# Another order for 1634 steps: linear attention and SwiGLU on one core

## The chip, the core and the metric

The kernel runs on one core of a Trainium2 chip. Six instruction streams work beside each other: TensorE (PE, with PEld for its weight loads), VectorE (DVE), ScalarE (ACT), GpSimd (POOL) and SyncE (SP), which here issues nearly all DMAs. The metric is the device time of one execution in microseconds. Three runs of the kernel before took 539.15 to 539.32 us, with a median of 539.2.

## The reference

Two stages are computed, the second from the first's output:

```python
def _attn_ref(q, k, v, alpha):                 # q, k, v, alpha: (4, 8, 768, 48)
    state = np.zeros((B, H, D, D), dtype=np.float32)
    for t in range(S):
        state = alpha[:, :, t, :, None] * state + np.einsum('bhd,bhe->bhde', k[:, :, t], v[:, :, t])
        y[:, :, t] = np.einsum('bhd,bhde->bhe', q[:, :, t], state)
    return y

def _moe_ref(x, w_gate, w_val, w_out):         # weights are float64: 384 x 1536, 384 x 1536, 1536 x 384
    g = x @ w_gate
    silu = g * (1.0 / (1.0 + np.exp(-g)))
    return (silu * (x @ w_val) @ w_out).astype(np.float32)

def reference(...):
    attn_out = _attn_ref(q, k, v, alpha)
    x = attn_out.transpose(0, 2, 1, 3).reshape(3072, 384)
    return _moe_ref(x, moe_w_gate, moe_w_val, moe_w_out)
```

## The kernel before

**Stage one: gated linear attention.** The 3072 tokens are 16 units of 192 tokens (four to a batch), each with all 8 heads, and a unit has three chunks of 64 tokens. For a unit u the loads La, Lk, Lq bring alpha, k and q and V*u*.i the values. The first units are turned on PE (T*, out of a copy widened by p*: pa, pk, pq), later ones by VectorE (tr, tk, tq). G and f are scans along time (backward and forward, lines 471 and 480). mk multiplies k by the backward scan (line 889 or 892), q multiplies q by the forward one into the tile X (line 496), and qc copies X's odd rows. K turns k for the chunks (PE, line 521), kc copies it (ACT, lines 525 and 526). C is a chunk's running sum (PE, line 597, the tile A), and ad copies it into V for the next chunk (line 620). S are the scores (PE, line 565), ma masks them (line 606), Y gives the output (PE, lines 658 and 659). From unit 4 on one step Z does scores, carry and the output of the unit before. yh and yl split the output into a high and a low part, and xr moves both into the tile xT by DMA: ten pieces a unit (line 745). xT holds 384 tokens, that is two units.

**Stage two: the MLP.** The tokens are 8 blocks of 384, d_ff is 12 slices of 128; a step s is one block and one slice, 96 in all. g and v are the two products (PE, line 760, nine matmuls each, since each operand is a high and a low part and three of the four products are taken), sl is the silu (ACT), h the product of both (DVE), hh and hl split it (ACT; then line 781 on DVE or POOL), and o adds into three banks of output rows (PE, line 793, nine matmuls). At a block's end ot copies three tiles of rows out of PSUM (line 805) and os stores them (line 818); the very last tile is stored by ACT (oz, line 809).

**Weights and checks.** Weights arrive as 64-bit words: wl loads a group, v0 to v2 cut it to 32 bits (line 162 on ACT), a and p split it. wr loads a weight slice again (384 KB) and wc checks its range; Lc and ck do so with alpha. The verdict is a flag, and behind the main path each engine loads it (line 1131) and branches to a general path that isn't taken here.

**What sets the order.** A string ORDER holds one word a step: the engine's letter (t PE, v DVE, s ACT, g POOL, y SP), the step's name, and behind @ the numbers of the PSUM banks that it takes. A loop walks it under a manual schedule:

```python
for word in ORDER.split():
    e, name = word.split(":")
    name, *banks = name.split("@")
    todo.pop(name)(engines[e], *(BANKS[int(x)] for x in "".join(banks)))
```

So each engine's queue, the buffers that the pools hand out, and the eight semaphores on which SP's transfers report in turn all follow from the order of the words. Nothing else is scheduled: an instruction waits at the head of its queue until its inputs and buffers are there.

Of the kernel before, what the change touches and what calls it, by code (L numbers as in the profile page):

```python
# [44 lines left out]
s:first y:La0 s:pa0 y:wl0 v:w0v0 t:Ta0@53 v:w0v1 s:ea0 y:Lq0 s:pq0 t:Tq0@03 v:G0 y:La1 y:V0.2 v:w0v2 s:pa1 v:f0 y:Lk1  # L45
s:pk1 t:Ta1@41 y:Lk0 t:Tk1@75 g:pk0 v:q0 s:ea1 y:V0.1 y:La2 y:Lq1 t:Tk0@60 v:mk0 y:wl1 y:V0.0 y:V0.3 s:ek1 s:pq1
t:K0.0@6 s:pa2 v:G1 s:kc0.0 g:w0a t:K0.1@4 t:Tq1@25 t:K0.2@6 v:mk1 t:C0.0@3 y:V0.4 s:w1v0 s:kc0.1 s:ad0.0 s:cq1 v:f1
g:w0p g:qc0 t:K1.2@7 t:C0.1@1 y:V0.5 t:S0@24 v:w1v1 v:ma0.1 v:ma0.0 y:wl3 v:ma0.2 y:V1.1 s:ad0.1 s:kc0.2 g:vc0 s:w3v0
t:C0.2@0 t:K1.1@3 t:K1.0@5 g:q1 y:La3 y:wl2 y:Lq2 s:ad0.2 v:de1 s:kc1.1 s:qc1 v:w3v1 v:w2v0 t:Y0@62 v:w1v2 t:S1@40
# [1114 lines left out]
```

## Time and profile before

| | us |
|---|---|
| median of three runs | 539.2 |
| the profiled execution | 539.45 |
| its span (first to last instruction) | 537.6 |
| PE busy | 525.5 (98%) |
| DVE busy | 398.7 (74%) |
| ACT busy | 244.8 (46%) |
| POOL busy | 138.8 (26%) |

The span is what the trace shows of the profiled execution; the 1.85 us by which its time is longer lie around it. Busy times count an engine's own work; the engines run beside each other, so the sums overlap. The costliest groups on PE are the MLP's: g 166.2, v 166.5 and o 257.4 us (160.5 with hh and 96.9 with hl). In the rows further down, "idle before" is the time in which the engine stood still just ahead of an instruction, and the arrow names what ended it.

### The profile page before, as it was taken

The page shows a single profiled execution, that of the slowest core. Times are in us where ns is not written, and L with a number is a line of the kernel's source. Part 1 is how long each engine was busy: PE and PEld are TensorE (multiplying, and loading weights), DVE is VectorE, ACT ScalarE, POOL GpSimd, SP SyncE. Part 2 cuts the span into 40 slices and gives each one's busy share as a digit, 9 for nine tenths or more (in the row PEclk, how much of TensorE's full clock was granted, in tenths as well). Part 3 has the DMA queues.
Part 4 walks back from the last instruction along what each step waited for, and adds up shares of the span by engine and source line. Part 5 has one row for each costly group of instructions (what it writes and reads, how often), then busy time and mean ns, then how long its engine had stood idle before and what let it go on. Part 6 is the DMA issues. An engine that isn't in the chain of part 4 may idle for free.

```text
span 537.6 us, 13527 instructions
## 1 busy us (share of the span) xinstructions
PE 525.5 (98%) x5346; PEld 514.2 (96%) x5346; DVE 398.7 (74%) x767; ACT 244.8 (46%) x573; POOL 138.8 (26%) x140
## 2 busy tenths in 40 slices
PE   5999999999999999999999999999999999999997
PEld 4789999999999999999999999999999999999996
DVE  7999999999999988988788777879856564212223
ACT  4999744443222234333242634533345553355333
POOL 8524143465233242101412014201012120110000
PEclk9999999999999999999999999999999999999999
DMA  8899767557358475765515757356264542424101
GB/s 241 222 314 243 200 194 219 135 132 202 86 145 227 101 183 125 184 156 131 147 44 145 186 132 197 82 144 176 66 164 132 140 109 62 134 53 119 52 1 48
DMA packets 96178, 77.60 MB, mean 144 GB/s; under 512 B 33264, under 2 KB 93040, under 8 KB 96112
## 3 DMA queue, kind: packets, MB, share of 16 engines
q1 hardware_dynamic: 95968, 76.52, 54.0%
q8 instruction: 43, 0.70, 0.6%
q14 instruction: 23, 0.19, 0.1%
q10 hardware_dynamic: 144, 0.20, 0.1%
HBM read 62.52 MB, written 5.90 MB: 127 GB/s over the span
## 4 chain that ended last, share of the span: by engine, by line
PE 95%; ACT 2%; DMA 1%; issue 0%; SPq 0%; DVE 0%; ACTq 0%
PE ops L793 28%; PE v L760 28%; PE g L760 28%; PE s L565 2%; PE c L680 2%; PE pt L418 1%; PE y L658 1%; PE y L659 1%; PE c L584 1%; DMA Le<-in_q_dram 1%; PE kps L521 1%; PE y L680 1%; PE A L597 1%; ACT V L620 0%; PE xp L731 0%
## 5 line engine op out<-in xcount | busy, mean ns | idle before, releaser
L760 PE MATMUL v<-xT,w 128*128 128x384 f32 x864 | 166.5, 336 | 0.0
L760 PE MATMUL g<-xT,w 128*128 128x384 f32 x864 | 166.2, 336 | 0.0
L793 PE MATMUL ops<-w,hh 128*128 128x384 f32 x576 | 160.5, 336 | 0.0
L760 PEld LDWEIGHTS v<-xT,w 128*128 128x128 f32 x864 | 150.8, 188 | 0.7 <-issue 0.3
L760 PEld LDWEIGHTS g<-xT,w 128*128 128x128 f32 x864 | 150.8, 188 | 0.3
L781 POOL TENSOR_TENSOR hl<-h,hh 128x384 fp32r<-128x384 f32 x58 | 61.8, 1067 | 275.8 <-ACT hh L776 269.6
L772 DVE TENSOR_TENSOR h<-h,v 128x384 f32<-128x384 f32 x96 | 53.1, 553 | 98.5 <-PE v L760 82.8
L793 PEld LDWEIGHTS ops<-w,hh 128*128 128x128 f32 x576 | 105.7, 188 | 0.3
L768 ACT ACTIVATE h<-g 128x384 f32<-128x384 f32 x96 | 47.0, 489 | 128.3 <-PE g L760 102.5
L776 ACT CAST hh<-h 128x384 fp32r<-128x384 f32 x96 | 48.9, 511 | 111.9 <-DVE h L772 59.8
L793 PE MATMUL ops<-w,hl 128*128 128x384 f32 x288 | 96.9, 336 | 0.0
L540 DVE STREAM_TRANSPOSE K<-Gs 32x192 f32<-32x192 f32 (+1 forms) x192 | 67.9, 353 | 4.7 <-POOL Gs L892 1.2
L793 PEld LDWEIGHTS ops<-w,hl 128*128 128x128 f32 x288 | 54.1, 188 | 0.0
L346 POOL TENSOR_TENSOR w<-t,w 128x768 fp32r<-128x768 f32 (+1 forms) x15 | 25.4, 1699 | 37.7 <-ACT w L342 37.6
L606 DVE TENSOR_TENSOR X<-s,mask 64x384 f32<-64x384 f32 (+1 forms) x48 | 26.4, 552 | 5.2 <-PE s L565 4.5
L480 DVE TENSOR_TENSOR_SCAN AT<-AT,back 128x771 f32<-128x771 f32 x16 | 29.2, 1827 | 0.6
L471 DVE TENSOR_TENSOR_SCAN Gs<-AT,inj 128x772 f32<-128x772 f32 x16 | 28.4, 1774 | 0.2
L781 DVE TENSOR_TENSOR hl<-h,hh 128x384 fp32r<-128x384 f32 x38 | 21.6, 574 | 8.9 <-ACT hh L776 8.5
L319 ACT ACTIVATE wc<-wc,wbias 128x384 f32<-128x384 f32 x36 | 23.4, 649 | 1.2
L629 DVE TENSOR_TENSOR V<-c,V 48x96 f32<-48x96 f32 x84 | 21.3, 254 | 1.9
L496 POOL TENSOR_TENSOR X<-trq,AT 112x768 f32<-112x768 f32 x9 | 15.6, 1737 | 25.5 <-DMA xT<-X 14.8
L892 POOL TENSOR_TENSOR Gs<-trk,Gs 128x768 f32<-128x768 f32 x9 | 15.3, 1697 | 23.1 <-DVE Gs L471 11.5
(121 smaller groups left out, 525.4 us busy)
## 6 DMA issues: line engine op xcount, KB each, us to landing
xT<-X SPq DMA_DIRECT2D x84, 72.0 KB, 2.2
raw<-in_moe_w_gate_dram SPq DMA_DIRECT2D x12, 384.0 KB, 4.7
raw<-in_moe_w_val_dram SPq DMA_DIRECT2D x12, 384.0 KB, 5.9
raw<-in_moe_w_out_dram SPq DMA_DIRECT2D x12, 384.0 KB, 5.7
wc<-in_moe_w_val_dram SPq DMA_DIRECT2D x12, 384.0 KB, 3.6
wc<-in_moe_w_gate_dram SPq DMA_DIRECT2D x12, 384.0 KB, 4.1
wc<-in_moe_w_out_dram SPq DMA_DIRECT2D x12, 384.0 KB, 3.6
ac<-in_alpha_dram SPq DMA_DIRECT2D x16, 288.0 KB, 3.7
```

The source lines that it names most:

```text
L319: nc.scalar.activation(dev, dev, AF.Relu, bias=wbias, scale=-1.0, accum_out=wviol[:, 0, i : i + 1])
L346: eng.tensor_tensor(out=lo, in0=src, in1=hi.bitcast(F32), op=ALU.subtract)
L471: nc.vector.tensor_tensor_scan(*(x.rearrange("p g t -> p (g t)")[:, ::-1] for x in (Gs, AT, inj)), 0.0, op0=ALU.mult, op1=ALU.add)
L480: nc.vector.tensor_tensor_scan(Af, Af, back[:, 1 : n + 1], back[:, 0:1], op0=ALU.mult, op1=ALU.add)
L540: nc.vector.transpose(out=bass.AP(k0.tensor, k0.offset, [k0.ap[0], (G * 2 * D, nc_), (2 * D, GF), (1, 32)]), in_=Kg[j * BO + x : j * BO + ...
L606: nc.vector.tensor_tensor(out=X[r, z, f * GF : (f + 1) * GF, :].rearrange("r g (c t) -> r g c t", c=NU), in0=sps[f][r].rearrange("r g (c t ...
L760: nc.tensor.matmul(pt, wsp[kind, f][a][:, kt * P : (kt + 1) * P], xT[blk][:, b_, kt, :], start=(n == 0), stop=(n == 3 * KT - 1),)
L768: nc.scalar.activation(h, acc.pop(("g", blk, f)), AF.Silu)
L772: nc.vector.tensor_tensor(out=h, in0=h, in1=acc.pop(("v", blk, f)), op=ALU.mult)
L776: nc.scalar.copy(out=hh, in_=acc["h", blk, f])
L781: eng.tensor_tensor(out=hl, in0=acc.pop(("h", blk, f)), in1=hh.bitcast(F32), op=ALU.subtract)
L793: nc.tensor.matmul(ops[blk][i], h[b_][:, i * P : (i + 1) * P], wsp["o", f][a], start=(first and n == 0), stop=(last and n == 2),)
```

## The change

Only ORDER differs. It has the same 1634 steps, in another sequence from the first word on. 73 steps stand on another engine: hl 37 (18 from POOL to DVE, 19 back), ot 13 (8 from DVE to ACT, 5 back), qc 9, the weights' a and p steps 6, mk 3, q 3, pa0 from ACT to DVE and pq1 from ACT to POOL. 43 steps take other PSUM banks, nearly all in the first 60 us; beside those Z7 and the last count, cp.

```diff
@@ ORDER, its first words
-s:first y:La0 s:pa0 y:wl0 v:w0v0 t:Ta0@53 v:w0v1 s:ea0 y:Lq0 s:pq0 t:Tq0@03 v:G0 y:La1 ...
+s:first y:La0 y:wl0 v:pa0 v:w0v0 y:Lq0 y:La1 t:Ta0@52 s:ea0 y:Lk1 y:V1.5 s:pq0 t:Tq0@54 ...
...
@@ ORDER, its last words
-v:h95 v:fl t:o94 s:hh95 v:hl95 t:o95 s:ot95.1 s:ot95.2 s:oz v:ot95.0 y:os95.0 t:cp@6 y:os95.1 v:fg
+v:fl t:o94 s:hh95 v:hl95 t:o95 v:ot95.1 s:ot95.2 s:oz y:os83.1 s:ot95.0 y:os95.0 t:cp@2 y:os95.1 v:fg
```

**PE in unit 0's chain**, from the first turned K on (before) and from the scores on (after). kps is k turned for a chunk, A_0_c the running sum of unit 0's chunk c, s_0 its scores, pt_2 the turned q, and the two Gs tiles are unit 0's (165, 171) and unit 1's (225, 233). Before:

```order
L521 MATMUL kps_0_219<-ident,Gs_165 64x112 x4
L521 MATMUL kps_1_231<-ident,Gs_165 64x112 x4
L418 MATMUL pt_2_0_236<-ident,wide 128x128 x3
L418 MATMUL pt_2_1_240<-ident,wide 128x128 x3
L521 MATMUL kps_2_244<-ident,Gs_165 64x112 x4
L597 MATMUL A_0_0_250<-V_80,K_104 48x48 x8
L521 MATMUL kps_2_274<-ident,Gs_225 64x112 x4
L597 MATMUL A_0_1_279<-V_80,K_104 48x48 x8
L565 MATMUL s_0_289<-X_102,Gs_165 64x64 x2
L565 MATMUL s_0_290<-X_102,Gs_165 64x64 x2
```

After:

```order
L565 MATMUL s_0_238<-X_102,Gs_171 64x64 x2
L565 MATMUL s_0_239<-X_102,Gs_171 64x64 x2
L597 MATMUL A_0_0_264<-V_80,K_104 48x48 x8
L418 MATMUL pt_2_0_276<-ident,wide 128x128 x3
L418 MATMUL pt_2_1_280<-ident,wide 128x128 x3
L521 MATMUL kps_2_291<-ident,Gs_171 64x112 x4
L597 MATMUL A_0_1_298<-V_80,K_104 48x48 x8
L521 MATMUL kps_0_307<-ident,Gs_233 64x112 x4
L597 MATMUL A_0_2_325<-V_80,K_104 48x48 x8
L521 MATMUL kps_2_334<-ident,Gs_233 64x112 x4
```

The scores stand ahead of the first running sum, where they stood behind the second, and the turned q (pt_2) has moved behind that first sum.

**SP between 137 and 146 us of the trace of before**: the ten pieces that move unit 4's output (X0) into block 2's tile xT2. V0 are values, wc17 and wc29 check loads, part0_2 a partial output read back, out_0 the output. The brackets name the semaphores that a row waits for; DMAHW*n* is one of the eight that count SP's transfers. Before:

```order
L745 DMA xT2_2133<-X0_102 16x2x192 [waits DMAHW1_49,DVE_49,PE_49]
L745 DMA xT2_2133<-X0_102 48x2x192 [waits DMAHW2_49]
L745 DMA xT2_2133<-X0_102 48x2x192 [waits DMAHW3_49,DVE_49]
L745 DMA xT2_2133<-X0_102 16x2x192 [waits DMAHW4_49]
L442 DMA V0_80<-in_v_dram 64x3x48 [waits DMAHW5_49]
L442 DMA V0_80<-in_v_dram 64x3x48 [waits DMAHW6_49]
L745 DMA xT2_2133<-X0_102 48x2x192 [waits DMAHW7_49]
L745 DMA xT2_2133<-X0_102 48x2x192 [waits DMAHW0_49]
L745 DMA xT2_2133<-X0_102 32x2x192 [waits DMAHW1_49]
L745 DMA xT2_2133<-X0_102 32x2x192 [waits DMAHW2_49]
L745 DMA xT2_2133<-X0_102 48x2x192 [waits DMAHW3_49,DVE_49]
L745 DMA xT2_2133<-X0_102 48x2x192 [waits DMAHW4_49]
```

After, the last seven of the ten pieces and what stands between and around them:

```order
L823 DMA part0_2_2146<-scratch_61 128x384 [waits DMAHW4_49]
L442 DMA V0_80<-in_v_dram 64x3x48 [waits DMAHW5_49]
L302 DMA wc17_2149<-in_moe_w_gate_dram 128x3x256 [waits DMAHW6_49]
L745 DMA xT2_2140<-X0_102 16x2x192 [waits DMAHW7_49]
L745 DMA xT2_2140<-X0_102 48x2x192 [waits DMAHW0_49]
L745 DMA xT2_2140<-X0_102 48x2x192 [waits DMAHW1_49,DVE_49]
L745 DMA xT2_2140<-X0_102 16x2x192 [waits DMAHW2_49]
L818 DMA out_0_dram<-part0_1_1862 128x384 [waits DMAHW3_49,DVE_49]
L745 DMA xT2_2140<-X0_102 32x2x192 [waits DMAHW4_49]
L745 DMA xT2_2140<-X0_102 48x2x192 [waits DMAHW5_49,Activation_49]
L745 DMA xT2_2140<-X0_102 48x2x192 [waits DMAHW6_49]
L302 DMA wc29_2190<-in_moe_w_gate_dram 128x3x256 [waits DMAHW7_49]
```

Between the pieces stand the check load wc17 and a store now, and the last piece waits for DMAHW6, on which wc17 reports.

**ACT at the end of the program.** hh_11 is the last high part, ot_i_11 the copies of the last block's three tiles of output rows, ops their PSUM banks. Before:

```order
L776 CAST hh_11_6887<-h_11_6847 128x384
L805 COPY ot_1_11_6900<-ops_1_0_6500 128x384
L805 COPY ot_2_11_6902<-ops_2_0_6501 128x384
L809 DMA out_dram<-ot_2_11_6902 128x384
L1131 TENSOR_LOAD flag
```

After:

```order
L776 CAST hh_11_6885<-h_11_6843 128x384
L805 COPY ot_2_11_6900<-ops_2_0_6508 128x384
L809 DMA out_dram<-ot_2_11_6900 128x384
L805 COPY ot_0_11_6905<-ops_0_0_6506 128x384
L1131 TENSOR_LOAD flag
```

ACT has tile 0 in place of tile 1, and copies it behind the store of tile 2; DVE copies tile 1 instead of tile 0.

**SP at the end.** ot7_0 and ot7_1 are those tiles, TENSOR_LOAD and ISA the load of the flag and what goes with it. Before:

```order
L455 DMA ac2_6713<-in_alpha_dram 128x2x288 [waits DMAHW3_49,Activation_49]
L818 DMA out_0_dram<-ot7_0_11_6905 128x384 [waits DMAHW4_49,DVE_49]
L818 DMA out_0_dram<-ot7_1_11_6900 128x384 [waits Activation_49]
L1131 TENSOR_LOAD flag_60 [waits DVE_49]
L1131 ISA x2
L1132 COMPARE_AND_BRANCH
```

After:

```order
L816 DMA out_0_dram<-ot6_1_11_6460 128x192
L816 DMA out_0_dram<-ot6_1_11_6460 128x192 [waits DMAHW3_49]
L1131 TENSOR_LOAD flag_60 [waits DVE_49]
L1131 ISA x2
L818 DMA out_0_dram<-ot7_0_11_6905 128x384 [waits Activation_49]
L818 DMA out_0_dram<-ot7_1_11_6898 128x384 [waits DVE_49]
L1132 COMPARE_AND_BRANCH
```

The two stores stand behind the load of the flag, where they stood ahead of it.

## Rows read from the trace of the kernel before

**Rows 1.** Page part 1: busy us, share of span, instructions of each engine.

```profile
PE 525.5 (98%) x5346; PEld 514.2 (96%) x5346; DVE 398.7 (74%) x767; ACT 244.8 (46%) x573; POOL 138.8 (26%) x140
```

**Rows 2.** What PE waited for: us in total, times, longest.

```profile
PE pt L418 <- POOL mask L243: 5.2, 1, 5.2
```

**Rows 3.** Windows of PE: stretch, us, busy (instructions), clock, DMA share.

```profile
10.00:35.00 25.00, 23.44 (x435) 1.00 0.93 252
```

**Rows 4.** Timeline, first loads: start, us, engine, operation, [idle before].

```profile
7.46 0.67 ACT L406 COPY wide<-Le 128x576 f32<-128x576 f32 x1 [0.17 <-DMA Le<-in_q_dram]
...
8.18 5.38 PE L418 MATMUL pt<-ident,wide 128*128 128x128 f32 x24 [1.49 <-ACT wide L406]
```

**Rows 5.** Timeline of the end, PE and ACT.

```profile
533.22 0.34 PE L793 MATMUL ops<-w,hh 128*128 128x384 f32 x1
...
534.10 0.38 ACTq L809 DMA_DIRECT2D out_dram<-ot  x1
```

**Rows 6.** Tile ot from 515 us on: ns min/median/max, starts.

```profile
L805 ACT COPY ot<-ops x2: 479/480/480, 533.1 to 533.6; 128x384 f32<-128x384 f32 x2
L818 SPq DMA_DIRECT2D out_dram<-ot x2: 357/375/393, 533.1 to 533.6; - x2
...
DMA to landing us min/median/max: 1.9/2.0/2.0
```

**Rows 7.** Source line 1131, the load of the flag, on SP.

```profile
L1131 SPq SEQ_ASSERT  x1: 33/33/33, 534.9 to 534.9; - x1
```

**Rows 8.** Page part 5, the subtraction hl on both engines: busy, mean ns, idle.

```profile
L781 POOL TENSOR_TENSOR hl<-h,hh 128x384 fp32r<-128x384 f32 x58 | 61.8, 1067 | 275.8 <-ACT hh L776 269.6
...
L781 DVE TENSOR_TENSOR hl<-h,hh 128x384 fp32r<-128x384 f32 x38 | 21.6, 574 | 8.9 <-ACT hh L776 8.5
```

**Rows 9.** Timeline of PE, unit 0.

```profile
14.22 0.96 PE L521 MATMUL kps<-ident,Gs 112*64 112x112 f32 x8 [0.65 <-DVE Gs L889]
...
16.41 0.56 PE L597 MATMUL A<-V,K 64*48 64x48 f32 x16
...
19.56 0.90 PE L597 MATMUL A<-V,K 128*48 128x48 f32 x16 [0.32 <-ACT K L525]
```

**Rows 10.** Timeline of ACT in the same stretch.

```profile
15.75 0.66 ACT L162 ACTIVATE t<-raw,lbias 128x384 f32<-128x384 uint32 x1
...
17.01 0.65 ACT L620 COPY V<-A 48x192 f32<-48x192 f32 x2
```

**Rows 11.** Timeline of SP, 136 to 163 us.

```profile
137.25 2.64 SPq L745 DMA_DIRECT2D xT<-X  x4
...
141.29 4.40 SPq L745 DMA_DIRECT2D xT<-X  x6
...
152.82 7.32 SPq L745 DMA_DIRECT2D xT<-X  x10
```

**Rows 12.** Timeline of POOL, the same stretch.

```profile
147.50 1.70 POOL L496 TENSOR_TENSOR X<-trq,AT 112x768 f32<-112x768 f32 x1 [2.56 <-DMA xT<-X]
```

**Rows 13.** Timeline of PE, the same stretch.

```profile
151.21 0.90 PE L565 MATMUL s<-X,Gs 48*64 48x64 f32 x48
...
162.14 1.02 PE L760 MATMUL g<-xT,w 128*128 128x384 f32 x5
```

**Rows 14.** DMA issues: KB each, median us to landing.

```profile
wc<-in_moe_w_gate_dram SPq DMA_DIRECT2D x12, 384.0 KB, 4.1
...
out_dram<-ot SPq DMA_DIRECT2D x14, 192.0 KB, 3.0
```

**Rows 15.** Tile wc, 150 to 152 us, one check load.

```profile
DMA to landing us min/median/max: 6.0/6.0/6.0
```

**Rows 16.** Source line 745, 136 to 163 us.

```profile
L745 SPq DMA_DIRECT2D xT<-X x20: 591/606/1062, 137.3 to 159.5; - x20
...
DMA to landing us min/median/max: 1.9/2.2/4.1
```

**Rows 17.** Source line 496, POOL's multiply.

```profile
L496 POOL TENSOR_TENSOR X<-trq,AT x9: 1689/1701/2041, 19.0 to 435.4; 112x768 f32<-112x768 f32 x9
```

More of the change, by code (lines that the diff above doesn't have):

```diff
@@ L44 @@
 ORDER = """
[L45 to L49, printed above, removed]
@@ L140 @@
-s:wc18 s:sl89 s:hh88 t:o87 t:v89 v:hl88 t:g91 v:h89 y:wr33 y:wr24 t:v91 s:hh89 s:sl91 v:h91 g:hl89 t:o88 t:g90 t:o89
-s:sl90 t:v90 s:hh91 v:h90 v:hl91 s:hh90 y:Lc2 t:g92 s:sl92 v:hl90 t:v92 t:o90 t:g94 v:h92 t:v94 s:ck2 s:sl94 s:hh92
-v:h94 g:hl92 t:g93 t:o91 s:hh94 s:sl93 t:o92 t:v93 v:h93 t:g95 t:v95 s:hh93 s:wc24 v:hl93 s:sl95 s:wc33 t:o93 v:hl94
-v:h95 v:fl t:o94 s:hh95 v:hl95 t:o95 s:ot95.1 s:ot95.2 s:oz v:ot95.0 y:os95.0 t:cp@6 y:os95.1 v:fg
+s:first y:La0 y:wl0 v:pa0 v:w0v0 y:Lq0 y:La1 t:Ta0@52 s:ea0 y:Lk1 y:V1.5 s:pq0 t:Tq0@54 y:Lk0 y:V0.0 s:pa1 v:w0v1 v:G0
@@ new lines @@
+y:wr0 y:Lq9 y:xr7.1 y:xr7.2 v:kr9.1 s:wc29 s:hh32 s:sl33 t:v33 g:hl32 v:h33 v:kr9.2 y:wr26 y:V9.6 t:g34 t:o31 t:v34
+v:kr9.0 s:sl34 v:tq9 s:wc17 s:hh33 t:g35 t:o32 y:wr19 y:V9.1 v:h34 v:hl33 v:ad8.1 v:q9 t:v35 s:sl35 y:Lk10 s:wc0
+s:hh34 v:h35 v:hl34 t:o33 t:g36 s:hh35 s:sl36 y:wr15 y:V9.2 y:V9.3 t:o34 t:v36 t:g37 v:hl35 v:tk10 v:h36 s:wc19 s:wc26
+y:V9.4 y:V9.5 t:o35 s:hh36 y:wr9 v:tr10 v:kr9.3 s:ot35.1 s:ot35.2 s:sl37 v:ad8.2 t:v37 t:Z9@20714 t:g38 s:wc15
+y:os35.2 s:yh8.0 s:ot35.0 v:h37 v:yl8.0 v:hl36 v:G10 y:os35.1 y:Lq10 s:yh8.1 s:sl38 s:yh8.2 v:ma9.2 t:v38 v:yl8.2
@@ new lines @@
+v:h48 t:v49 v:tk12 v:ot47.0 y:Lq12 s:hh48 s:wc35 s:sl49 v:ad11.1 v:ma11.1 y:xr10.0 y:os47.0 y:wr4 s:wc27 s:yh10.1
+s:yh10.2 v:h49 v:ot47.1 g:hl48 t:g50 t:v50 s:ot47.2 v:mk12 s:sl50 s:hh49 v:hl49 t:o48 t:g51 y:wr5 y:Lc14 s:wc5 v:h50
+v:tq12 v:yl10.1 s:hh50 t:v51 s:sl51 v:yl10.2 v:h51 t:o49 v:hl50 y:V12.1 y:wr11 t:g52 t:v52 v:kr12.0 v:f12 s:hh51
+s:sl52 t:g53 t:o50 y:V12.7 y:xr10.2 v:hl51 s:wc11 s:qc11 v:h52 y:xr10.1 s:hh52 s:sl53 y:V12.5 y:os47.2 v:kr12.2
+v:ma11.0 t:o51 t:v53 v:hl52 v:h53 y:V12.2 s:hh53 t:g54 t:o52 t:v54 y:Lk13 s:sl54 s:wc4 t:g55 g:hl53 v:h54 y:V12.3
@@ new lines @@
+t:o74 v:kr15.1 g:q15 t:g76 v:kr15.2 t:v76 g:hl75 s:sl76 v:h76 g:qc15 s:wc6 s:hh76 y:wr13 v:hl76 t:g77 s:sl77
+t:Z15@21560 t:o75 s:yh14.0 v:yl14.0 s:yh14.1 s:yh14.2 s:wc13 t:v77 y:Lc10 v:yl14.2 v:ma15.2 v:ma15.0 v:ad15.0 v:ma15.1
+v:h77 s:ck12 s:hh77 t:o76 t:v78 t:g79 v:ad15.1 v:h78 v:yl14.1 t:Y15@21 y:Lc13 s:yh15.0 s:hh78 v:hl77 g:hl78 t:v79
+s:sl79 y:xr14.0 v:h79 t:o77 t:g81 t:v81 s:hh79 s:wc20 s:sl81 y:xr14.1 y:xr14.2 y:Lc4 t:g80 v:h81 t:o78 v:yl15.0
+s:yh15.1 t:v80 v:hl79 s:sl80 s:hh81 v:hl81 v:yl15.1 v:h80 t:g82 t:o79 t:v82 s:sl82 s:ck10 s:hh80 s:ck4 v:h82 g:hl80
```

172 lines of the change are left out of this document (82 added, 90 removed).

## The prediction

> **What bounds the kernel now.** I read the page first. Its first part shows TensorE (PE) busy for 525.5 of the span's 537.6 us [rows 1]. So the time is the PE's own work plus the little that stands before, inside and behind it. The profiled execution took 539.45 us, 1.85 us more than its span; the three timed runs have a median of 539.2. I work in differences and put them on 539.2. About 0.2% (1.1 us) is what a measurement of this kernel can tell from no change.
>
> Next I read who kept the PE waiting. The list has five entries, the longest 5.2 us at the very start [rows 2], and all five lie in the first 35 us. The busy time shows what that is after the first loads: from 10 to 35 us the PE works 23.44 of 25.00, so it lacks 1.56 us [rows 3]. Before that it waits for the first two loads: the second group of transposes starts at 8.18, behind a load of q and a 0.67 us copy on ScalarE (ACT) [rows 4]. After 35 us the list names no wait. VectorE (DVE) is 74% busy, ACT 46%, GpSimd (POOL) 26% [rows 1]: they cost time only where a PE instruction comes before they are done. Last I read the end, in order of time [rows 5, 6, 7].
>
> A new order can therefore win at most those 1.56 us; it can lose at three kinds of places: the start, a new wait in the middle, and the tail behind the last matmul.
>
> **The change part by part.** The matmuls are the same, so the PE's own work is the same.
>
> Of the 73 changes of engine 37 are the subtraction hl: 18 go from POOL to DVE, 19 from DVE to POOL. One costs 1067 ns on POOL and 574 on DVE [rows 8], so the net of one is +1.07 us on POOL and -0.57 on DVE, and the POOL sat idle 275.8 us ahead of its hl's. The copies of outputs (ot: 8 to ACT, 5 to DVE, 0.48 us each on ACT [rows 6]) go to an engine with half its time free. The other 23 are of the same kind (products, copies and weight cuts of a unit). I cost all these at nothing; the cover is that idle time, and where it is missing one move costs the 0.5 us by which POOL is slower.
>
> The start. The first widening copy goes from ACT to DVE. The trace has no such copy on DVE; DVE's subtraction of 384 columns takes 574 ns [rows 8], which bounds it by 0.57 and, if it grows with the columns, by 0.57 x 576/384 = 0.86. ACT takes 0.67, so the first transposes move by -0.10 to +0.19 us. That is hidden, because the second group still waits for the same load of q, third in its queue before and after [rows 4]. Then unit 0's chain: k turned, copied by ACT, multiplied (A_0_0, A_0_1, A_0_2), each sum copied by ACT before the next. Before, A_0_0 starts at 16.41 and A_0_2 at 19.56 [rows 9]. After, the scores of unit 0 (s_0, 0.90 us by those of unit 6 [rows 13]) fill the PE until some 14.22 + 0.96 + 0.90 = 16.1, and A_0_0 can start there, 0.3 earlier. But ACT has more between A_0_0 and A_0_2 than before: a weight cut (0.66 us) and the two copies of q, 0.5 each by a copy of that size [rows 6]. A_0_0 ends near 16.6; the two copies of its sums (0.65 a pair) end at 17.5 behind the cut [rows 10], the q copies at 18.5, the next pair of K copies, which are as long a row, at 19.1, the pair for A_0_1 at 19.8. A_0_2 starts there, 0.2 later. What was won is given back. Bounds: -1.56 (every wait gone) and, by the same size, +1.6; I take 0, and 0.7 to either side as likely.
>
> The middle. Between 137 and 146 us the SyncE queue (SP) issues ten pieces that move unit 4's result into xT2, with two other loads among them: 12 rows from 137.25 to 141.29 + 4.40 = 145.69, 0.70 each [rows 11]. POOL's multiply for unit 6 waits for the last piece (it overwrites the same X0): it starts at 147.50, 1.81 behind the last issue, and takes 1.70 [rows 12]. The scores of unit 6 start at 151.21 [rows 13], 2.0 after it ended. After, the same ten pieces have six other rows among them, one the 384 KB load of a weight check (wc17), one a store. Each transfer reports on one of eight counters in turn, and the rows of the order show the last piece waiting for the counter of wc17, eight rows ahead. By the pace alone the 16 rows end at 137.25 + 16 x 0.70 = 148.45. By the counter: wc17 is the eighth, issued near 142.15, and lands 4.1 us later (median of such loads [rows 14]) or 6.0 (the one of this stretch [rows 15]); the last piece is issued at 146.3 to 148.2 and ends by 148.85. So the multiply starts at 150.26 to 150.66 and ends at 151.96 to 152.36, and the scores are 0.8 to 1.2 late. If a row takes the 0.61 us of a bare issue [rows 16], they are not late. Take 0.6, the middle.
>
> A second path ends at block 2's first product (g), at 162.14 [rows 13]. It waits for the last piece of unit 5, whose issue ends at 152.82 + 7.32 = 160.14 [rows 11]: 2.0 us, and a piece takes 2.2 to land [rows 16], so nothing is to spare. After, ten rows follow the late last piece (4.7 us), and one of them waits for a second check load (wc29, issued near 148.9, landed at 153.0 to 154.9). So the first row that the pieces stand behind goes out at 153.5 to 155.8, the next 11 end at 161.3 to 163.6, and the last lands at 162.9 to 165.2: g is 0.8 to 3.0 late, with the 0.6 of the first place in it. At bare pace and with both loads at 4.1 it is 0. I take 0.9, near what the median landing gives, for both places together; 0 and 3.0 stay as ends. Nothing gives that back, since the PE is never idle later.
>
> The row of POOL's multiply has one of nine at 2041 ns and a median of 1701 [rows 17]. The Trainium skill (GPSIMD Engine Reference, 1. Specifications) says that GpSimd shares its SBUF interfaces with VectorE and contends with DVE instructions that read two tensors from SBUF. The one long row agrees, the other eight do not show it; by the rule the first place would be 0.34 later and the sum 0.3 us higher.
>
> The tail. Before, the last matmul ends at 533.22 + 0.34 = 533.56 [rows 5]. DVE copies the first third of the last rows, ACT the other two [rows 6]. SP issues the first two stores from 533.1 on [rows 6], and ACT the third at 534.10 [rows 5]. A store takes 2.0 us to land [rows 6], so the last lands at 536.1, and the span ends 1.5 behind it. After, DVE copies the second third. ACT copies the third, issues its store (534.10 to 534.48), and only then copies the first: 534.52 to 535.00, by the 0.48 us of such a copy [rows 6]. SP has the load of the flag and its two register steps ahead of the two stores, where they stood behind them; in the trace of before these are done at 534.93 [rows 7], and the flag's value, which the load waits for, is ready no sooner after. That is hidden behind ACT's copy by 0.07 us or more; were ACT sooner, this would hold the stores. So the first store goes out at 535.03 and the second, long ready but queued behind it, at 535.45 (issues of 0.36 to 0.39 us [rows 6]). It lands at 537.45, and the span ends 1.5 later: 538.95 in place of 537.6, **+1.35 us**. Bounds: +1.2 with landings of 1.9; +2.35 with the 3.0 of the stores in mid-kernel [rows 14]. I take 2.0, since these stores run in the same quiet stretch.
>
> **The sum.** Start 0, middle +0.9, tail +1.35: +2.25 us, 541.7 for the profiled execution and 541.45 on the median; I say 541.5.
>
> **The rivals.**
> First: the middle is not late, because the check loads land in about 4 us and SP issues at the bare pace. For it: the median landing of such loads is 4.1 [rows 14]. Against it: the one check load of that very stretch took 6.0 [rows 15]. Then only the tail counts: 539.2 + 1.35 = 540.55.
> Second: both check loads take 6 us or more, and the whole queue shifts. The middle costs 3.0: 539.2 + 3.0 + 1.35 = 543.55. For it: rows 15; against it: the median landing.
> Third, on the other side: unit 0's chain. If ACT runs s_0's and A_0_0's copies as early as the PE allows, all 1.56 us of idle PE between 10 and 35 us go, and the queue is early enough in the middle. 539.2 - 1.56 + 1.35 = 539.0, no slower. It decides from a gain of about 0.3 us on, below which the whole is slower than 0.2%. For it: A_0_0 is 0.3 earlier. Against it: ACT's extra 1.6 us between A_0_0 and A_0_2 [rows 6, 10]. Faster by over 0.2% it is only if the tail is hidden as well, for which no row speaks: 537.6.
>
> **How the numbers follow.** The forecast gets 0.52, the first rival 0.21, the second 0.10, the third 0.17, since the start is where my working is least sure. All of the forecast and of the second rival is slower; of the first, a third (0.07) wins a little at the start as well and ends within 0.2%; of the third, 0.10 is the same and 0.07 faster. So slower 0.52 + 0.14 + 0.10 = 0.76, same 0.17, faster 0.07. The low end, 539.0, is the third rival's time; the high end, 543.6, is the second's. The forecast by itself spans 540.8 to 542.6, with 0.7 of the start to either side and half a microsecond of the middle.
>
> **What would show it.** Tail: in the profile after, some 3.9 us from the last matmul's end to the last landing, where 2.5 stood, and SP's stores behind the flag's load. Middle: POOL's multiply of unit 6 released by a transfer of xT near 150, and PE waits near 151 and 163 that the list of before lacks. Start: the PE's sum of idle time from 10 to 35 within 0.7 us of 1.56. I am wrong if the PE's last matmul ends no later than before with the waits absent, or if the last store goes out before 534.6.

## The result, and the profile after

The changed kernel takes 546.02 us (median of five runs, 545.33 to 547.67) where the kernel before took 539.23 beside it: a ratio of 1.0128 with a 95% interval of 1.0111 to 1.0146. It is slower, as forecast, but by 6.8 us and not by 2.3. The time lies outside the stated range.

The profiled execution took 545.33 us with a span of 543.6, 6.0 more than the span of before. The rows that answer to [rows 1], from the page:

```profile
PE 526.7 (97%) x5346; PEld 514.4 (95%) x5346; DVE 394.8 (73%) x760; ACT 246.5 (45%) x578; POOL 147.6 (27%) x142
```

PE does the same 5346 matmuls, with 1.2 us more of busy time. Neighbouring matmuls overlap (each row lasts 0.2 us or more, and the next one of a dense group starts 0.02 us behind it), so a short wait inside a group counts as busy; what is lost is therefore read below from the moments at which the same work is done. What PE waited for (the view of [rows 2]: us in total, times, longest):

```profile
PE pt L418 <- POOL mask L243: 5.4, 1, 5.4
PE s L565 <- POOL X L496: 1.2, 1, 1.2
PE pt L418 <- ACT wide L406: 1.2, 1, 1.2
PE A L597 <- DMA L<-in_alpha_dram: 0.8, 1, 0.8
PE kps L521 <- DVE Gs L889: 0.8, 1, 0.8
PE pt L418 <- ACT K L526: 0.4, 1, 0.4
PE v L760 <- DVE h L772: 0.2, 1, 0.2
```

The second and the last are new and lie at 153 and 178 us, where the list of before had nothing. Three moments at which PE has done the same work in both kernels show where the time went: the second row of unit 6's burst (c, line 680), its scores (s), and the scores of unit 7. First the timeline of PE before, from 150 and 177 us:

```profile
150.48 0.92 PE L680 MATMUL c<-X,V 48*64 48x64 f32 x48
...
177.89 0.90 PE L565 MATMUL s<-X,Gs 48*64 48x64 f32 x48
```

Then the same of the changed kernel:

```profile
151.27 0.92 PE L680 MATMUL c<-X,V 48*64 48x64 f32 x48
153.40 0.93 PE L565 MATMUL s<-X,Gs 48*64 48x64 f32 x48 [1.20 <-POOL X L496]
...
181.28 0.90 PE L565 MATMUL s<-X,Gs 48*64 48x64 f32 x48
```

At c the changed kernel is 151.27 - 150.48 = 0.79 us late, at unit 6's scores 2.19 (153.40 against the 151.21 of [rows 13]), at unit 7's 3.39. Its last matmul ends 3.39 late too (536.61 + 0.34 against 533.56). So in this execution all that the body (all ahead of the last matmul's end) lost was lost by 181 us, and on balance nothing was lost or won in the 355 us behind that. The other 2.6 us lie behind the last matmul: 543.6 - 536.95 = 6.65 us against 537.6 - 533.56 = 4.04.

**The start.** From 10 to 35 us (the columns of [rows 3]):

```profile
10.00:35.00 25.00, 22.77 (x432) 1.00 0.91 255
```

PE lacks 2.23 us where it lacked 1.56. The moments of the same work show where it fell behind. The rows of the changed kernel (timeline of PE, from A_0_2 and from 25 us):

```profile
19.69 0.90 PE L597 MATMUL A<-V,K 128*48 128x48 f32 x16 [0.82 <-DMA L<-in_alpha_dram]
...
25.24 0.87 PE L418 MATMUL pt<-ident,wide 128*128 128x128 f32 x6 [0.43 <-ACT K L526]
```

Ahead of A_0_2 PE has done the same 132 matmuls in both kernels, and it starts 0.13 us late (19.56 in [rows 9]). The row names a load of alpha as what ended the wait; by time it is ACT's copy of the sum before, which starts at 19.32, and in a_tail, a_xr4, a_s3 and b_early the view names that copy. Ahead of the transposes at 25.24 (24.56 before) PE waits for a K copy on ACT and is 0.68 late. A wait of before, which [rows 2] leaves out, is gone behind that:

```profile
PE pt L418 <- DVE Y L709: 0.4, 1, 0.4
```

At 31 us the lateness is down to 0.29. It is 0.60 at 51.5, behind a wait inside the scores of unit 3 (below), and 0.79 from 92 us to c.

**The middle.** SP from 143 us, then POOL (the views of [rows 11] and [rows 12]):

```profile
143.69 3.44 SPq L745 DMA_DIRECT2D xT<-X  x4
147.22 0.53 SPq L818 DMA_DIRECT2D out_dram<-part  x1
147.79 1.94 SPq L745 DMA_DIRECT2D xT<-X  x3
```

```profile
151.66 1.69 POOL L496 TENSOR_TENSOR X<-trq,AT 112x768 f32<-112x768 f32 x1 [6.86 <-DMA xT<-X]
```

The last piece's issue ends at 149.73, POOL starts 1.93 later, and the scores start 0.05 behind POOL's end: the 2.0 us of slack are used up, and PE stands 1.2 us. (wc17, on whose counter the last piece waits, landed at 148.44, and that piece's turn came at 149.13.)

**The tail.** Timeline of DVE, PE, ACT and SP at the end, and the landing time of the two stores from tile ot (the views of [rows 5] and [rows 6]):

```profile
536.47 0.56 DVE L805 COPY ot<-ops 128x384 f32<-128x384 f32 x1 [1.33 <-PE ops L793]
536.61 0.34 PE L793 MATMUL ops<-w,hh 128*128 128x384 f32 x1
...
536.99 0.48 ACT L805 COPY ot<-ops 128x384 f32<-128x384 f32 x1 [2.56 <-PE ops L793]
...
537.50 0.38 ACTq L809 DMA_DIRECT2D out_dram<-ot  x1
537.97 0.48 ACT L805 COPY ot<-ops 128x384 f32<-128x384 f32 x1 [0.51 <-ACT ot L805]
538.48 0.81 SPq L818 DMA_DIRECT2D out_dram<-ot  x2
```

```profile
DMA to landing us min/median/max: 3.1/3.1/3.1
```

The order is as forecast, and so are the issues: in time from the last matmul's end the first late store goes out at 538.48 - 536.95 = 1.53 (forecast 535.03 - 533.56 = 1.47). But it lands after 3.1 us, not 2.0. The DMA view of that stretch, by queue, shows what ran beside it: 539.3 to 541.6 in the changed kernel,

```profile
q1 hardware_dynamic: 288, 0.39, 51.5%
q14 instruction: 3, 0.02, 3.5%
```

and 533.9 to 535.74, the time of the three stores, before:

```profile
q1 hardware_dynamic: 288, 0.39, 60.0%
q10 hardware_dynamic: 144, 0.20, 29.6%
q8 instruction: 1, 0.02, 3.3%
```

Behind the branch on the flag code is loaded. Three 8 KB loads of it (q14) run from 539.45 to 540.9 among the late stores' packets, and a 16 KB one (q8) from 538.96 to 540.07. Behind 540.5 only 31 of these 256 packets are left, but they go out one by one until 541.5, at a busy share of two or three of the 16 DMA engines. Before, the same loads began at 535.7 (q8) and 535.9, when the stores' packets were out. All other traces agree: SP's two stores landed 2.8 to 3.5 us behind their issue in each of the nine with the changed end, and 1.9 to 2.0 in each of the nine with the end of before. That the loads of code hold the stores is read from the order in time; no run has the one without the other.

### The profile page after: what moved, and what is told of

The parts are those of the page before. It is cut to its first block, busy times and chain, and to the rows that moved or that the text cites. A ratio compares the mean times of both kernels' runs of the same rounds, so it can differ in the third digit from the quotient of the medians.

```text
span 543.6 us, 13544 instructions
## 1 busy us (share of the span) xinstructions
PE 526.7 (97%) x5346; PEld 514.4 (95%) x5346; DVE 394.8 (73%) x760; ACT 246.5 (45%) x578; POOL 147.6 (27%) x142
## 4 chain that ended last, share of the span: by engine, by line
PE 89%; SPq 3%; DVE 3%; ACT 1%; DMA 1%; issue 1%; POOL 1%; ACTq 0%; DVEq 0%; POOLq 0%
PE ops L793 26%; PE v L760 26%; PE g L760 26%; PE pt L418 2%; PE s L565 2%; PE c L680 2%; SPq L745 2%; PE y L658 1%; PE y L659 1%; PE c L584 1%; PE y L680 1%; PE A L597 1%; SPq L442 1%; SPq L390 1%; DMA L<-in_q_dram 1%
## 5 line engine op out<-in xcount | busy, mean ns | idle before, releaser
L781 POOL TENSOR_TENSOR hl<-h,hh 128x384 fp32r<-128x384 f32 x59 | 65.4, 1110 | 271.1 <-ACT hh L776 266.9
L781 DVE TENSOR_TENSOR hl<-h,hh 128x384 fp32r<-128x384 f32 x37 | 20.5, 553 | 19.8 <-ACT hh L776 19.7
L496 POOL TENSOR_TENSOR X<-trq,AT 112x768 f32<-112x768 f32 x12 | 20.5, 1708 | 35.8 <-DVE trq L398 16.4
L892 POOL TENSOR_TENSOR Gs<-trk,Gs 128x768 f32<-128x768 f32 x8 | 13.6, 1695 | 33.3 <-DVE Gs L471 30.1
```

The lines of the kernel that those rows point to most:

```text
L781: eng.tensor_tensor(out=hl, in0=acc.pop(("h", blk, f)), in1=hh.bitcast(F32), op=ALU.subtract)
```

## The experiments

Sixteen more runs followed, each beside the kernel before on its chip. Their medians, and what they lie above the kernel before there:

| kernel | median us | above before |
|---|---|---|
| the change | 546.0 | +6.8 |
| a_tail, b_tail | 544.8, 541.7 | +5.9, +2.9 |
| a_xr4, a_early | 550.9, 544.1 | +12.1, +5.3 |
| a_again (the change once more) | 547.8 | +8.6 |
| a_wr17, a_xr4b, a_fix | 548.1, 549.8, 544.0 | +8.9, +10.6, +4.8 |
| a_fix2, b_early, b_mid, a_s3 (one run) | 544.3, 541.8, 543.1, 548.7 | +5.4, +3.0, +4.2, +9.9 |
| a_half, a_half_tail | 543.2, 541.1 | +4.3, +2.3 |
| b_k2, b_best | 539.7, 540.8 | +0.8, +1.9 |

The three moments of the same work, read in the traces, separate start and middle. At unit 6's c the kernels with the changed start are late by 0.8 (the change), 0.9, 1.0, 2.6, 3.0, 3.6 and 4.7 us (a_tail, a_wr17, a_s3, b_early, a_xr4b, a_again); those with the start of before, b_k2 and b_best left aside, lie within 0.4 of before. From there to unit 7's scores the six with the changed middle (the change, a_again, a_tail, a_early, a_wr17, a_s3) lose 2.4 to 4.0 us; the six with the middle of before (a_half, a_half_tail, b_tail, b_early, b_k2, b_best) lose nothing. So the start is what differs most from one execution to the next. Behind unit 7's scores the first six lose 0.0 to 0.8 us more. (a_xr4 is left out: it stood 5.2 us just ahead of c.)

**a_tail and b_tail: the end alone.** What differs, the last words (b_tail has them the other way round, on the kernel before):

```diff
-t:o95 v:ot95.1 s:ot95.2 s:oz y:os83.1 s:ot95.0 y:os95.0 t:cp@2 y:os95.1 v:fg
+t:o95 y:os83.1 s:ot95.1 s:ot95.2 s:oz v:ot95.0 y:os95.0 t:cp@6 y:os95.1 v:fg
```

> The changed kernel with the last nine words of the kernel before (DVE copies tile 0, ACT tiles 1 and 2, both stores ahead of the flag's load on SP); all else is the changed kernel's. Theory (the tail costs 2.6 us: 1.35 by the copies' and stores' order, 1.2 by landings of 3.1 us in place of 2.0, because late stores meet the load of the code behind the branch): from the last matmul's end to the span's end 4.0 us where the changed kernel has 6.7, and 2.6 us less time, some 543.4 for a median of 546.0. Rival one (only the order costs, the long landings are there either way): 1.35 less, 544.7, and landings of 3 us stay. Rival two (the end of the span is set by something else, the code load itself): no gain, 546.0.

> The kernel before with the end of the changed kernel (DVE copies tile 1, ACT tile 2, its store and then tile 0, SP loads the flag ahead of both stores); all else is the kernel before. Theory: 2.6 us more than before, 541.8, with the two last stores landing 3 us after their issue while code is loaded. Rival one (1.35 by the order alone): 540.6 and landings of 2.0. Rival two: no difference, 539.2.

b_tail: 541.73, ratio 1.0055 [1.0042, 1.0069], 2.9 us more, near the 2.6. Its stores (tile ot) landed as in the changed kernel, the early one of ACT in 1.9 and the two late ones in 3.0 us:

```profile
L818 SPq DMA_DIRECT2D out_dram<-ot x2: 347/388/428, 534.8 to 535.2; - x2
...
DMA to landing us min/median/max: 1.9/3.0/3.0
```

a_tail's trace has 4.0 us behind the last matmul, as expected, and landings of 2.0. But its time did not show the 2.6 (1.0113 [1.0098, 1.0129] against 1.0128): its body, the changed kernel's to the last o product, ended its last matmul at 538.6 where the profile of the changed kernel has 536.95. That was the first sign that the body's loss differs from one execution to the next.

**a_again: the changed kernel once more.**

> The changed kernel once more, word for word, for its body's spread: its five runs lay between 545.3 and 547.7. Theory (the stalls of its body hang on how long SP's rows and landings take in an execution): the wait at unit 6's scores is between 1.0 and 2.5 us in the trace, and the time 5 to 8 us above before. Rival (one fixed loss): the wait is 1.2 and the time within 0.5 of 6.8 us above before in every run.

547.80 us (546.40 to 549.76), 1.0148 [1.0131, 1.0166]: the loss is no fixed one, but my theory named the wrong place. PE's wait at unit 6's scores was 0.8 us, below the 1.0 to 2.5 that I expected, and the time is 8.6 us above before, beyond the 5 to 8: PE was 4.7 us late ahead of SP's rows. Its list of waits has a new row,

```profile
PE s L565 <- issue: 1.8, 1, 1.8
```

and the timeline of PE shows it in the middle of one instruction group, the 48 scores of unit 3:

```profile
51.83 0.46 PE L565 MATMUL s<-X,Gs 48*64 48x64 f32 x15
54.08 0.73 PE L565 MATMUL s<-X,Gs 48*64 48x64 f32 x33 [1.80 <-issue]
```

"issue" is a wait for nothing that the profile shows. A 16 KB load of code (queue q8) ended at 52.60, 1.48 us before PE went on. Counted over PE's matmuls in the traces, the wait stands right behind the 717th in the two runs of the change, in a_tail, a_wr17, a_xr4b and b_early (from the start of the matmul ahead of it 0.29, 2.02, 0.92, 0.37, 0.36 and 0.37 us) and behind the 718th in a_s3, always 1.4 to 1.6 us behind the end of such a load; an earlier one stands behind the 215th (0.30 to 2.07 us in the change, a_xr4, a_xr4b, a_s3 and b_early), 1.3 to 1.5 us behind one. a_xr4, with the same start, has none behind its 717th. The kernel before has 0.26 us behind its 219th (a_fix, with that start, 0.59) and none above 0.15 near its 700th. PE takes 96 instructions for the 48 scores, in 0.9 us; the reading is that it comes there to the end of the code that it has. No row shows the fetch itself. The Trainium skill (Runtime: NRT & Kernel Launch, Instruction fetch mechanics) says that an engine's code is refilled in blocks of 16 KiB while it executes, and that crossing into the next block is mostly hidden. The size agrees; that it is hidden does not hold for these dense groups, by up to 2.1 us, if the reading is right.

Behind a longer wait the granted clock can fall too: in windows of a_again (stretch, us, PE busy, clock, DMA share),

```profile
54.00:56.00 2.00, 1.92 (x51) 0.83 0.29 80
56.00:58.00 2.00, 2.00 (x8) 0.50 0.23 56
```

0.50 is the lower level, 1.2 GHz: a product's matmul takes 0.32 us there instead of 0.18, and ten of them cost 1.5 us more. The same trace has the clock at 0.50 from 14.3 to 17.8 us too, behind waits of 1.2, 0.6 and 1.0 us at 8.1, 12.3 and 14.4.

**a_s3: the scores one product earlier.**

```diff
-t:g2 t:v2 t:C3.0@1 t:S3@24 t:C3.1@1
+t:g2 t:S3@24 t:v2 t:C3.0@1 t:C3.1@1
```

> The changed kernel with one word moved: the scores of unit 3 (96 instructions in 1 us) one product earlier on PE, ahead of v of step 2 (18 instructions in 1.6 us). Theory (PE waits there for its next 16 KB of code, whose landing does not depend on where PE stands): PE comes to the end of its code 1 us earlier or more, and the wait in the middle of the scores grows to 1.3 us or more, still 1.4 to 1.5 us behind the end of a 16 KB load of code. Rival (the wait is one for a tile of the scores, a bank or X, that the profile doesn't show): the scores wait at their first matmul or not at all, for some 0.2 us.

The amount was wrong: 0.5 us and not 1.3, since the load of code also came earlier (it ended at 49.33, not at 50.03). The place speaks for the theory and against a tile: the words moved, the wait stayed at the same count of PE's instructions, so it has gone further into the scores:

```profile
49.78 0.82 PE L565 MATMUL s<-X,Gs 48*64 48x64 f32 x41
50.89 0.34 PE L565 MATMUL s<-X,Gs 48*64 48x64 f32 x7 [0.29 <-issue]
```

**a_early and b_early: the start alone.** a_early is the first 345 words of the kernel before, then the changed kernel's; b_early the reverse.

```diff
-s:first y:La0 y:wl0 v:pa0 v:w0v0 y:Lq0 y:La1 t:Ta0@52 ...
+s:first y:La0 s:pa0 y:wl0 v:w0v0 t:Ta0@53 v:w0v1 s:ea0 ...
```

> The changed kernel with the start of the kernel before: its first 345 words, up to the tenth g product, then all other words in the changed kernel's order. Theory (the start costs 0.8 us at 98 us of the span, and what comes later is its own): block 2's first g 0.8 us earlier, 545.2. Since the stall at unit 6's scores is set by SP's queue and not by PE, rival one: SP's pieces do not come earlier, the stall there grows by what PE gained, and nothing is won: 546.0. Rival two (the start sets the pace of the queue and so all later stalls): 2 us or more less, 544.0.

> The kernel before with the start of the changed one: its words up to the tenth g product, then the rest in the order of the kernel before. Theory (the start costs 0.8 us by A_0_2 and more where PE's code comes late at the scores of unit 3, near 51 us): 0.8 to 2.5 us more than before, with an unexplained wait (issue) at those scores in the trace, 1.4 to 1.5 us behind the end of a 16 KB load of code. Rival (the start is given back later, as I forecast): within 0.5 us of before.

a_early: 544.09, 1.0095 [1.0080, 1.0111], 1.8 us better than the change by the two ratios, though their intervals touch; I expected 0.8. Its trace has the middle alone: at c PE is 0.15 us ahead of before (150.33), at unit 6's scores 1.17 behind (152.38), at unit 7's 2.65 (180.54). b_early: 541.84, 1.0049 [1.0035, 1.0062], 3.0 us worse than before where I expected 0.8 to 2.5. So the start costs some 1.8 to 3.0 us of the median, and is not given back. In b_early's profiled execution, the slowest of its five, the waits in the middle of a group are 1.1 (behind the 215th) and 0.4 us (717th), the K copy's wait costs 0.5, and PE is 1.8 us late by 53 us; two new waits of 0.7 and 0.6 us at 92 and 367 us, for a copy ot and for nothing shown, came on top.

**b_mid: the middle alone.**

```diff
-y:xr4.1 y:V6.4 y:V6.2 y:xr4.0 y:xr4.2 y:V6.6 y:os18.2 y:V6.0 y:pl18.0 y:Lk7 y:wr29
+y:xr4.1 y:V6.4 y:V6.2 y:V6.6 y:V6.0 y:wr8 y:wr29 y:xr4.0 y:xr4.2 y:os18.2 y:pl18.0 y:Lk7
```

> The kernel before with four rows more on SP among unit 4's pieces: the check loads wc8 and wc29 and two loads of values, all moved ahead of its second third. Theory (rows of 0.65 us and a piece's issue held behind a large load by 0.8 to 1.4 us): the last piece is issued 3.4 to 4.0 later, POOL's multiply with it, and the scores of unit 6 wait 1.3 to 2.0 us: 1.3 to 2.5 us more than before. Rival (the 2.0 us of slack there hide it): no difference.

543.06, 1.0074 [1.0060, 1.0087]. POOL's multiply starts at 150.00 instead of 147.50 and the scores wait:

```profile
151.74 0.93 PE L565 MATMUL s<-X,Gs 48*64 48x64 f32 x48 [0.63 <-POOL X L496]
```

With the 0.4 us wait of a v product at 175 that made the last matmul 1.0 us late: the mechanism is there, at less than I expected. The other part of the 4.2 us is none of it, and no accident of one execution, since all five runs lie 3.4 us or more above before: its stores landed 2.55 us behind the last matmul, as before, but the span ended 4.2 us after that and not 1.5. Behind its branch SP has eight steps to do (source line 1132). Before:

```profile
L1132 SPq EVENT_SEMAPHORE  x8: 17/17/17, 535.5 to 536.2; - x8
L1132 SPq COMPARE_BRANCH  x1: 70/70/70, 535.0 to 535.0; - x1
```

In b_mid:

```profile
L1132 SPq EVENT_SEMAPHORE  x8: 17/17/17, 539.4 to 539.9; - x8
L1132 SPq COMPARE_BRANCH  x1: 70/70/70, 536.3 to 536.3; - x1
```

SP stood 3.0 us between the branch and the first of them, where it had stood 0.4, and went on at the pace of before. What it waited for no row shows: the last store had landed at 537.07 and the last of four loads of code ended at 537.72, 1.6 us before SP went on. So this edit at 140 us came with a changed end too, for a reason that stays open.

**a_wr17, a_xr4, a_xr4b, a_fix, a_fix2: SP's rows put back.** The ten pieces stand closer in all five; the moves in SP's order:

```diff
a_wr17   wr17 from ahead of xr4.1 to behind xr4.2
a_xr4    xr4.1 xr4.2 V6.4 V6.5 V6.6 V6.1 V6.0 right behind xr4.0, ahead of pl18.2
a_xr4b   xr4.0 pl18.2 xr4.1 xr4.2 os18.1 V6.4 V6.5 V6.6 V6.1 V6.0 pl18.0 wr17 wr29
a_fix    a_xr4b, with the start and the end of the kernel before
a_fix2   a_fix, with wr17 wr29 wr8 behind xr5.2
```

> The changed kernel with one word moved: the check load wc17 stands behind the last of unit 4's pieces instead of ahead of the fourth. Theory (wc17's 384 KB hold the pieces behind it: one of them takes 1.4 to 2.0 us to issue in place of 0.6, and a row less stands ahead of the last): the last piece 1.4 to 2.0 earlier, and 1.0 to 1.6 us less time than the changed kernel on the same chip. Rival (a row is a row, of whatever size): 0.65 us less.

> The changed kernel with the ten pieces of unit 4's result behind one another on SP; the loads of values of unit 6 follow them directly, and the check loads wc17 and wc29, the part loaded back and the stores stand behind these. Theory (the last piece is late by rows on SP at 0.7 us each, which holds POOL's multiply and so the scores of unit 6): the last piece is issued by 145, POOL's multiply starts near 147.5, the scores' wait of 1.2 us and the 0.4 around it go, 1.6 us less time: 544.4. Rival (another input of that stage, the values of unit 6 or the end of the output's split, is late next): a wait of 0.5 us or more stays at the scores or the carry, and 1.0 us or less is gained.

> The changed kernel with unit 4's pieces behind one another on SP as before, but the load of the partial output (which the copy ot on DVE waits for) stays ahead of them, and the next such load stands ahead of the check loads wc17 and wc29. Theory (the last run of this kind lost 5.2 us because DVE waited for that load, not because of the pieces): no wait of a v product for h above 0.5 us, no wait of unit 6's scores for POOL, and 1.6 to 2.0 us less than the changed kernel. Rival (the next input is late instead): less than 0.8 us won, with a new wait between 150 and 180 us.

> The changed kernel with all three places put back: the start of the kernel before (345 words), the pieces as in the run with them together, and the end of the kernel before; the other thousand words are the changed kernel's. Theory (start 0.8, middle 1.8, tail 2.6 us, and nothing else of weight): within 1.0 us of before, 538.8 to 540.0 where before takes 538.8. Rival (the body has other losses that show once these are gone): 541 or more.

> The changed kernel with the start and the end of the kernel before, unit 4's pieces behind one another, and the three check loads wc17, wc29 and wc8 behind unit 5's last piece too (in the last run of this kind the stall moved to block 2's first two g products, 1.6 and 2.2 us for unit 5's pieces, and the clock fell to 0.50 behind them). Theory (SP's rows ahead of unit 4's and unit 5's pieces are what the middle costs): no wait of PE between 60 and 530 us above 0.5 us, the clock stays 1.00, and the time is within 0.8 us of before. Rival (thirty-odd rows are still too many ahead of unit 5's last piece): a wait of 1 us or more at block 2's g, and 541 or more.

a_wr17: the last piece was issued 0.63 us earlier, a row's worth, and the pieces were held as before (3.28 us for four): the size of wc17 is not what holds them. No time was won, neither my 1.0 to 1.6 us nor the rival's 0.65 (548.12, 1.0161 [1.0148, 1.0174], where a_again has 547.80 on the same chip); the carry of unit 6 now waited 0.8 us for its values.

In the other four the scores' wait for POOL is gone: in a_xr4 POOL's multiply starts at 147.82. What came instead cost PE more, each time another load of the same queue. In a_xr4 (550.92, 1.0244 [1.0222, 1.0266]) the partial output pl18.2 landed at 152.80, DVE stood for its copy, and PE waited 5.2 us for h (timeline of DVE, then windows of PE):

```profile
152.88 0.56 DVE L801 TENSOR_TENSOR part<-ops,part 128x384 f32<-128x384 f32 x1 [5.75 <-issue]
```

```profile
150.00:152.00 2.00, 0.00 (x0) 1.00 0.65 133
152.00:154.00 2.00, 0.00 (x0) 0.76 0.94 327
154.00:156.00 2.00, 1.58 (x5) 0.50 0.61 186
```

In a_xr4b (549.80, 1.0182 [1.0164, 1.0200]) and a_fix PE waited for unit 5's pieces, at two g products of block 2 (waits of PE in a_fix):

```profile
PE g L760 <- DMA xT<-X: 3.6, 2, 2.2
```

The granted clock fell to 0.50 for 6.8 us behind them. a_fix's profiled execution (546.68) is the slowest of its six. In a_fix2 the three check loads stood ahead of unit 7's q, for which DVE stood 4.1 us and PE, behind it, 2.8:

```profile
171.94 1.62 DVE L398 STREAM_TRANSPOSE trq<-L 128x768 f32<-128x768 f32 x1 [4.12 <-DMA L<-in_q_dram]
```

a_fix (543.96, 1.0077 [1.0061, 1.0093]) and a_fix2 (544.29, 1.0104 [1.0086, 1.0121]) refute my expectation that three places put back would give the time of before. Both traces run level with before, within 0.4 us, up to unit 6's scores: rows moved off one deadline stood ahead of the next.

**a_half and a_half_tail: the first 830 words of the kernel before, whole.**

```diff
-words 1 to the 38th g product in the changed kernel's order
+the same in the order of the kernel before; a_half_tail has its last nine words too
```

> The changed kernel with the order of the kernel before up to the 38th g product (830 of 1634 words, some 200 us), the rest and the end in the changed kernel's order. Theory (start, queue and code waits of the first 200 us are the whole body): the last matmul ends within 0.6 us of before, the tail costs 2.6, so 2.4 to 3.2 us more than before. Rival (the second half loses by its 40 moved splits and stores): 4 us or more above before.

> The same with the end of the kernel before as well; only the words between the 38th g and the last o product are the changed kernel's. Theory: within 0.6 us of before. Rival one (the second half has losses of its own): 1 us or more above. Rival two (the changed kernel's second half is the better one): 0.5 us or more below.

a_half: 543.17, 1.0084 [1.0070, 1.0098]. Its last matmul ends 0.8 us later than before's, which one wait at the seam accounts for, 1.1 us at 235 us for a copy of an output on ACT (waits of PE; the 38th g product is at 231 us, not at some 200 as I wrote):

```profile
PE y L658 <- ACT ot L805: 1.1, 1, 1.1
```

Neither kernel has that wait, so in this trace the changed order's second half loses nothing of its own. The time, 4.3 us above before, is nonetheless my rival's (4 or more) and not my 2.4 to 3.2: 0.8 at the seam and 2.3 behind the last matmul (6.3 us where it was 4.1) leave some 1.2 us of the median that the profile does not show. a_half_tail: 541.12, 1.0045 [1.0031, 1.0058], 2.05 us less by the end alone. I expected it within 0.6 of before; the 2.3 us that it lies above are the 0.8 at the seam, 1.0 between the last landing and the end of the span (2.5 where it was 1.5), and half a microsecond that its profiled execution does not show.

**b_k2 and b_best: the start of the kernel before.**

```diff
-t:Tk2@06 t:R0.2@2 t:R0.0@6      (b_k2; b_best also has y:wl0 v:w0v0 v:w0v1 behind y:Lq0)
+t:Tk2@02 t:R0.2@6 t:R0.0@7
```

> The kernel before with three other PSUM banks: the second half of unit 2's turned k takes bank 2 instead of 6, the repacks R0.2 and R0.0 banks 6 and 7 instead of 2 and 6. Theory (PE waits 0.4 us near 30.7 for DVE to empty bank 6, which no longer holds it): that wait goes and 0.3 to 0.5 us are won. Rival (the next wait, of a repack for its bank, takes its place): no difference.

> The same three banks, and the load of q ahead of the first weights' load on SP, with that weight's first two cuts on DVE behind it in the order. Theory (PE's second group of transposes waits 1.5 us for that load of q, which lands some 0.5 us earlier when 384 KB of weights do not go ahead of it): 0.3 to 0.6 us less than with the banks alone. Rival one (a later load of the start is late by the same): no more than the banks alone give. Rival two (the backward scan stands behind the cuts on DVE, which wait for the later weights): 0.3 us or more slower than the banks alone.

b_k2: 539.68, 1.0014 [1.0005, 1.0023], a little slower. The wait at 30.7 went to the repacks, as the rival had it (timeline of PE):

```profile
30.69 1.72 PE L731 MATMUL xp<-Y,sel 112*128 112x384 f32 x8 [0.30 <-ACT trq L865]
33.14 0.62 PE L731 MATMUL xp<-Y,sel 112*128 112x384 f32 x2 [0.72 <-ACT xT L735]
```

b_best: 540.78, 1.0041 [1.0027, 1.0055], 1.1 us slower than the banks alone: rival two, by its number and its mechanism. q landed at 5.04, but PE's second group started at 7.87, no earlier than in other runs with the start of before (7.80 to 8.36). What moved is DVE (its timeline, and POOL's):

```profile
7.91 1.78 DVE L471 TENSOR_TENSOR_SCAN Gs<-AT,inj 128x772 f32<-128x772 f32 x1
```

```profile
10.92 1.63 POOL L406 COPY wide<-Le 128x576 f32<-128x576 f32 x1 [1.21 <-PE pt L418]
```

The cut at 7.04 waits 2.9 us for the weights, and the backward scan stands behind it (7.91; 7.25 in b_k2). The forward scan then ran beside 1.17 us of POOL's copy of k, which took 1.63 us where it took 0.66 in b_k2 beside 0.16 us of scan, and PE's next group came 0.5 us later than before. No version beat the kernel before.

## Why the prediction was wrong

The direction and the three places were right; the sizes were not. In the profiled execution the start cost 0.79 and not 0, the middle 2.6 and not 0.9, the tail 2.6 and not 1.35; together 6.0 and not 2.25.

- **The ceiling** ("can win at most those 1.56 us") was not put to the test, since nothing was won. The 37 moved subtractions cost nothing that shows: no row of PE waits for hl, and from unit 7's scores on, with most of them ahead, PE lost nothing on balance.
- **The start** lacked a term. The chain that I worked out was right: A_0_0 at 16.15 (16.1), A_0_2 at 19.69 (19.8), 0.13 late with the same work done, and the idle time from 10 to 35 us is 0.67 more than before, within the 0.7. But I took the chain for the whole start. Behind it PE lost 0.5 at 25 us to a K copy of ACT, which I had not costed, and won 0.4 back at 31; the wait inside unit 3's scores, which I had at nothing and put down to code, gave 0.3, and 0.2 to 0.3 came by 92 us in steps too small for a row. It was this term that reached 2.0 in a_again: the list of before has none of it, since its one such wait (0.26) is too short for a row.
- **The middle, first place** was mis-sized. Pace, not the counter, set the last piece: 16 rows from 138.05 to 149.73, 0.73 each against my 0.70, begun 0.8 later than before; POOL started 4.2 us later than before, where I had 2.8 to 3.2 by the two workings and took less than either. So the scores came 2.2 late, 1.4 of it beyond what PE was late already. I took 0.6, halfway between my upper working of 1.2 and the bare issue, and had the pieces begin on time. The 0.34 us by the Trainium skill's rule (GPSIMD Engine Reference, 1. Specifications) did not come: the multiply took 1.69 us.
- **The middle, second place** did not come in the changed kernel: with PE already held at the scores, block 2's g found unit 5's pieces just there (the last landed at 165.36, and PE took it at 165.39 without a row of waiting). In a_fix, where the scores are not held, it is the bound: PE stood 3.6 us. I added two places that stand in for each other; behind the scores another 1.2 us went, to the carry, a v product at 177.68 and smaller gaps. My 4.7 us for ten rows between the two units' pieces also does not follow from rows of 0.70: they took 6.4 us, eleven rows.
- **The tail** had the right order and issues, to 0.1 us. The landing was wrong: I took 2.0 of "the same quiet stretch", but a stretch 1.5 us later has loads of code in it, and the stores landed after 3.1. My own upper bound (+2.35, by landings of 3.0) was near the +2.6 measured by luck, since its 3.0 is that of stores in mid-kernel.
- **The range** had no term that differs from run to run. The five runs of the kernel before beside the change lie within 0.6 us (eleven beside a_again within 1.3); those of the changed kernel spread over 2.3 to 3.4 us, and behind a longer wait the clock can fall as well (a_again). That is 0.7 us of the median, and more on the chip of a_again.

Of the rivals, the second (543.55) was nearest, by the sum and not by its mechanism: its two check loads took 5.4 and 3.6 us to land, and neither held a piece.

Left open: whether it is code that PE waits for inside its dense groups, and why that takes 0.3 us in one execution and 2.0 in the next; whether the loads of code hold the late stores, which no run separates; and what SP stood for at the end of b_mid.

## What to carry to other kernels

When an engine is 98% busy, a new order has little to win and every queue's slack to lose: list the deadlines of the DMA queue (each load and who waits for it) and move no row ahead of one without checking the next, since a row taken off one deadline stands ahead of another. To cost a tail, don't take a landing from a store that was issued before the program's end, and to see what a stage cost, compare the moments at which the same work is done, and not the idle time: at A_0_2 PE had waited 0.5 us more than before and was 0.13 late. A change that removes slack can show as a spread of the runs, so one profiled execution need not be the median: it was the fastest of five for the change and the slowest for a_again, b_early and a_fix.
